# Three more transposes handed to the DMA rings, loads that queue behind them, and a new instruction order in a fused attention and channel-mix kernel

## The chip, the cores and the metric

The kernel runs on one core of a Trainium2 chip. The metric is device time in microseconds (us), the median of several executions. A profiled execution gives the trace that is read below.

## What is computed

Cut to what matters (B = 8 batches, H = 8 heads, S = 576 tokens, head width 64, so C = 512; F = 1024):

```python
kv  = einsum('bhsd,bhse->bhde', k, v)
u   = einsum('bhsd,bhde->bhse', q, kv)
x   = u / sqrt(mean(u * u, axis=-1) + 1e-6) * g_norm          # heads side by side: (B, S, C)
x_prev = x shifted by one token (zero in front)
xk  = mu_k * x + (1 - mu_k) * x_prev
xr  = mu_r * x + (1 - mu_r) * x_prev
km  = maximum(xk @ w_k, 0)                                     # (B, S, F)
out = 1 / (1 + exp(-(xr @ w_r))) * ((km * km) @ w_v)           # (B, S, C)
```

Inputs and output are float32 in memory; the matmuls work on bfloat16.

## The kernel before

**Stages of one batch.** The three inputs of a batch come by DMA from the queue of GpSimd (POOL), cast on the way (`load`, L189 to L194; word `ld.0`, `ld.1`, `ld.2` for k, v and q). TensorE (PE) makes `kv` (word `kv`, L278 to L288), which ScalarE (ACT) or VectorE (DVE) moves out of PSUM (`kvo`). q must be turned so that its channels lie on the partitions. Up to batch 3 that is 36 small PE transposes for each half of the heads (`qt`, L322 to L330), moved out by `qto`; from batch `QD = 4` on it is one transposing DMA on the queue of SyncE (SP) (`q_turn`, word `qd`, L299 to L302). Such a batch needs a swapped copy of `kv` as well (`kvs`, L295), and its `u` is made from 64x64 pieces (`u_turned`, L304, products on L316) in place of `u` (L342, products on L352).

Then come the squares of u (ACT, `sq`, L357), their sums (DVE, `red`, L361), a Newton iteration for the inverse root (DVE, `nw`, eight short steps) and the product (DVE, `mul`). The normalised rows must be turned back to have channels on the partitions: up to batch 4 by 36 PE transposes (`x` and `x0`, L435) moved out by `xo` and `x0o` with the factor g_norm; for batches in `YD = (5, 6, 7)` the product goes into the one tile `yd` (`mult_rows`, L399 and L403), a transposing DMA on SP's queue writes the tile `xT` (`y_turn`, word `yd`, L407 to L409), and `gx` (L411) multiplies by g_norm in place.

`xT` feeds `wrap` (L591), `dif` (L595), the scaled differences `sc` (L601 on ACT, L603 on DVE) and the sums `add` (L618) that give xk and xr. Then the channel mix: `K` (L631, four matmuls 128x288 and a relu for each of 8 blocks and 2 halves), `ks` (the squares, L639 or L637), `R` (L653, then a sigmoid, L656), `V` (L663, a group of four matmuls 128x512), `fin` (DVE product L676, then two stores on SP's queue, L684). The channel mix takes 128 tokens at a time, across the border of a pair of batches.

**The order.** A scheduler is switched off (`tc.manual_schedule()`). The string `ORDER` lists every step as a word; the loop on L791 to L796 issues them one by one, and each engine and each DMA queue works through its own instructions in that order, waiting by semaphores where data or a buffer is not ready. A quote mark after a word puts the step on DVE, else ACT, where there is a choice; the digits after `=` name the PSUM banks that the step takes. A bank is taken by the matmuls and given back by the step that reads it out last.

**Buffers.** k and q of even batches, and v, go into fixed tiles (`sq0`, `q0`, `qT0`), so the next even batch's load waits until the last reader is done; odd batches share one tile for each input (`in_k`, `in_v`, `in_q`). Working tiles come from a pool that hands out buffers of a tag in rotation: two for each tag of `mine` (L264), seven for `rt` (L645), six for `sig` (L655), seven for `out` (L675).

**The head and the tail.** Batch 0 and batch 1 have words of their own (`kvc`, `uc`, `Ka`, `Kz` for batch 0; `kvh`, `uh`, `xh` for the two halves of batch 1's heads). The last 128 tokens are made by `last_vv` (L666, words `L.0` and `L.1`), 256 columns at a time, with a product and two stores (one on SP's queue, one on ACT's) for each.

## Time and profile before

| | |
|---|---|
| Median of 3 runs | 199.24 us (198.97 to 199.28) |
| The profiled execution's own time | 198.45 us |
| Its span, first to last instruction | 196.7 us |
| PE busy | 185.8 us (94%) |
| DVE busy | 163.0 us (83%) |
| ACT busy | 134.1 us (68%) |
| POOL busy | 27.6 us (14%) |
| Bytes moved by DMA | 31.51 MB, mean 160 GB/s |

Times in views of the trace count from the first instruction. A line such as `L631` is a line of the kernel before; a busy PE is one with matmuls in flight, not one at its peak. A DMA's landing is when its completion semaphore reaches its full count; the instruction that issues it ends long before, save that a transposing DMA keeps its queue's engine for some us.

### The profile page before, as it was taken

How to read it: one execution, taken by the hardware profiler on the slowest of the kernel's cores; microseconds unless marked ns; L12 is line 12 of the kernel's file. 1: busy time of each engine (PE TensorE's matmuls, PEld its weight loads, DVE VectorE, ACT ScalarE, POOL GpSimd, SP SyncE). 2: the span in 40 equal slices, each digit the busy share in tenths (PEclk: the TensorE clock that was granted, in tenths of full speed). 3: DMA queues.
4: the chain of work that ended last, by engine and by line, in shares of the span. 5: the costliest groups of instructions: out<-in, count | busy, mean ns of one | idle time of the engine just before them, and what ended most of it. 6: DMA issues, size and time to landing. Idle time of an engine off the chain costs nothing.

```text
span 196.7 us, 5776 instructions
## 1 busy us (share of the span) xinstructions
PE 185.8 (94%) x2387; PEld 111.1 (56%) x2409; DVE 163.0 (83%) x356; ACT 134.1 (68%) x275; POOL 27.6 (14%) x44
## 2 busy tenths in 40 slices
PE   7788899999999999999999999999999999999991
PEld 2435565665564667567554775676445666764450
DVE  2488899996999999978999899899899997876241
ACT  2375898779969867969987658989855557532310
POOL 7953343004021004002100000000000000000000
PEclk9999999999999999999999999999999999999999
DMA  5999999999999998999999378335723842005654
GB/s 212 219 211 206 202 205 208 207 217 243 230 230 208 220 189 223 224 170 268 154 215 202 81 136 171 86 80 29 176 45 58 182 107 57 0 0 130 140 144 124
DMA packets 38030, 31.51 MB, mean 160 GB/s; under 512 B 18924, under 2 KB 32500, under 8 KB 38004
## 3 DMA queue, kind: packets, MB, share of 16 engines
q0 software_dynamic: 14400, 16.19, 49.3%
q1 hardware_dynamic: 23204, 14.43, 33.5%
q10 hardware_dynamic: 400, 0.52, 0.8%
q8 instruction: 19, 0.31, 0.6%
q14 instruction: 7, 0.06, 0.1%
HBM read 33.56 MB, written 9.44 MB: 219 GB/s over the span
## 4 chain that ended last, share of the span: by engine, by line
PE 80%; DVE 9%; DMA 4%; issue 2%; ACT 2%; SPq 0%; DVEq 0%; POOLq 0%
PE ps_v L663 28%; PE ps_km L631 28%; PE ps_r L653 15%; DMA q<-in_q_dram 3%; PE ps_kv L287 2%; PE ps_u L316 1%; DVE y L420 1%; PE ps_x L435 1%; DMA out_dram<-out_sb 1%; DVE xT L512 1%; DVE out_sb L676 1%; PE ps_u L352 1%; DVE ss L361 1%; DVE sqk L639 1%; PE ps_qt L330 1%
## 5 line engine op out<-in xcount | busy, mean ns | idle before, releaser
L663 PE MATMUL ps_v<-wv_sb,sqk 128*128 128x512 bf16 x266 | 64.8, 379 | 1.0 <-issue 0.3
L631 PE MATMUL ps_km<-xk,wk_sb 128*128 128x288 bf16 (+3 forms) x480 | 64.0, 285 | 0.0
L631 PEld LDWEIGHTS <-wk_sb 128*128 128x128 bf16 x480 | 45.7, 98 | 16.2
L663 PEld LDWEIGHTS <-sqk 128*128 128x128 bf16 x280 | 26.7, 98 | 29.5 <-issue 0.6
L623 ACT ACTIVATE rt<-ps_km 128x288 bf16<-128x288 f32 (+3 forms) x81 | 33.5, 427 | 12.6 <-PE ps_km L631 9.0
L653 PE MATMUL ps_r<-wr_sb,xr 128*128 128x512 bf16 x136 | 34.9, 379 | 0.5
L656 ACT ACTIVATE sig<-ps_r 128x512 bf16<-128x512 f32 x36 | 21.2, 596 | 18.9 <-PE ps_r L653 18.6
L676 DVE TENSOR_TENSOR out_sb<-ps_v,sig 128x512 f32<-128x512 f32 (+1 forms) x37 | 24.3, 670 | 9.3 <-PE ps_v L663 7.7
L637 ACT ACTIVATE sqk<-rt 128x576 bf16<-128x576 bf16 (+4 forms) x32 | 23.4, 746 | 4.4 <-DVE rt L625 4.2
L601 ACT ACTIVATE m<-dx,cols 128x576 bf16<-128x576 bf16 (+1 forms) x30 | 21.7, 756 | 4.2 <-DVE dx L595 4.0
L625 DVE TENSOR_SCALAR rt<-ps_km 128x288 bf16<-128x288 f32 (+3 forms) x39 | 17.8, 473 | 6.6 <-PE ps_km L631 5.0
L653 PEld LDWEIGHTS <-xr 128*128 128x128 bf16 x144 | 13.9, 98 | 14.2
L361 DVE TENSOR_REDUCE ss<-sq 128x16 f32<-128x1024 bf16 (+1 forms) x12 | 15.8, 1344 | 0.4 <-ACT sq L357 0.4
L357 ACT ACTIVATE sq<-ps_u 128x512 bf16<-128x512 f32 (+1 forms) x30 | 14.6, 556 | 0.0
L618 DVE TENSOR_TENSOR xr<-m,xT 128x1152 bf16<-128x1152 bf16 x16 | 11.9, 750 | 0.8 <-ACT m L601 0.8
L639 DVE TENSOR_TENSOR sqk<-rt 128x576 bf16<-128x576 bf16 (+3 forms) x25 | 11.7, 482 | 0.7 <-ACT rt L623 0.6
L595 DVE TENSOR_TENSOR dx<-xT 128x2304 bf16<-128x2304 bf16 (+5 forms) x13 | 11.4, 893 | 0.4
L603 DVE TENSOR_SCALAR m<-dx,cols 128x576 bf16<-128x576 bf16 (+3 forms) x36 | 11.4, 346 | 0.2
L618 DVE TENSOR_TENSOR xk<-m,xT 128x1152 bf16<-128x1152 bf16 (+2 forms) x16 | 10.9, 699 | 0.2
L420 DVE TENSOR_TENSOR y<-ps_u,rs 128x512 bf16<-128x512 f32 (+1 forms) x15 | 8.4, 628 | 0.1
L217 ACT CAST kv<-ps_kv 128x128 bf16<-128x128 f32 (+1 forms) x15 | 3.3, 244 | 6.9 <-PE ps_kv L472 5.7
L261 PE MATMUL ps_warm<-zeros 128*128 128x512 bf16 x18 | 6.9, 502 | 1.2 <-DVE eps L224 1.2
(91 smaller groups left out, 162.2 us busy)
## 6 DMA issues: line engine op xcount, KB each, us to landing
out_dram<-out_sb SPq DMA_DIRECT2D x67, 128.0 KB, 3.2
qT<-in_v_dram POOLq DMA_DIRECT2D x3, 576.0 KB, 14.4
sq<-in_k_dram POOLq DMA_DIRECT2D x3, 576.0 KB, 12.9
q<-in_q_dram POOLq DMA_DIRECT2D x3, 576.0 KB, 10.8
in_q<-in_q_dram POOLq DMA_DIRECT2D x3, 576.0 KB, 7.9
in_v<-in_v_dram POOLq DMA_DIRECT2D x3, 576.0 KB, 14.3
in_k<-in_k_dram POOLq DMA_DIRECT2D x3, 576.0 KB, 11.8
wk_sb<-in_moe_w_k_dram POOLq DMA_DIRECT2D x2, 512.0 KB, 9.1
```

The source lines that it names most:

```text
L357: ACT.activation(out=sq[:, rg(t0, n, i) if n else slice(0, 1)], in_=held["u", a, part, i][1], func=AF.Square)
L361: DVE.tensor_reduce(out=ss[:, g0:g1], in_=sq[:, g0:g1], op=ALU.add, axis=AX.X)
L601: eng.activation(out=out_, in_=in_, func=AF.Copy, scale=mu)
L618: DVE.tensor_add(out=dst, in0=m[:, hs, c0:c1], in1=x[:, hs, c0:c1])
L623: eng.activation(out=dst, in_=ps, func=AF.Relu)
L625: eng.tensor_scalar(out=dst, in0=ps, scalar1=0.0, scalar2=None, op0=ALU.max)
L631: nc.tensor.matmul(ps[:, n, :], wk_sb[:, cc, 128 * fc:128 * fc + 128], at[b]["xk"][:, cc, c0:c1], start=(cc == 0), stop=(cc == NHP - 1))
L637: eng.activation(out=sqk[:, fcs, o:o + n], in_=src, func=AF.Square)
L653: nc.tensor.matmul(ps, xr[:, cc, 128 * t:128 * t + 128], wr_sb[:, cc, :], start=(cc == 0), stop=(cc == NHP - 1))
L656: ACT.activation(out=sig[b, t], in_=give("r"), func=AF.Sigmoid)
L663: nc.tensor.matmul(ps, sqk[:, fc, 128 * t:128 * t + 128], wv_sb[:, fc, :], start=(fc == 0), stop=(fc == NFC - 1))
L676: DVE.tensor_mul(out=o, in0=give(key), in1=sig[b, t][:, c])
```

## The change

Five things change together.

1. `QD` goes from 4 to 3 and `YD` from (5, 6, 7) to (4, 5, 6, 7): batch 3's q and batch 4's y are turned by DMA and not by PE.
2. Each transposing DMA leaves a piece of its output in a list `turning`. The next `load` first copies two values from each such piece on GpSimd, so it waits for the landing of the transposing DMAs that stand ahead of it in the order, and so do all loads behind it on that queue. (A step `gate` that did such a copy for q alone, and that the order before did not use, is gone.)
3. Work tiles get names of their own: one buffer each for even and odd batches, and slots for `rt`, `sig` and `out` that are taken from a list of free ones and returned by the step that used them last. The counts stay 7, 6 and 7.
4. `last_vv` splits its columns 384 and 128 in place of 256 and 256, and the order does the 128 first.
5. The whole order is new, with the banks. It has 22 filler matmuls (`wm` and the 12 at the start) where there were 18.

The diff, the order cut to the places that are spoken of:

```diff
-    Kz.0.2 Kz.0.0 Kz.0.5' ... Ka.0.7=7 ... Kz.0.6 ... qt.1.0=50 Kz.0.3' ... Kz.0.7 ... kvh.0=41 kvho.0.0 Kp.0.1.1'=3
-    kvho.0.1 Kp.0.1.0'=2 uh.1.0=60 ...
+    fu.0.0.1.0.256 Kz.0.2' Ka.0.5=7 fu.0.0.3.0.256 sc.0.1.0' kvh.0=30 qto.1.0.1 kvho.0.1' qto.1.0.0 Kz.0.5'
+    kvho.0.0 uh.1.0=52 uh.0.0=14 ...
...
-    kv.2=26 ... ld.2.4 ... ld.0.4 ... kv.3=37 ... ld.1.4 qt.3.1=40 ... qt.3.0=21 ... ld.2.5 ... ld.0.5 ... ld.1.5 ... qd.4
+    kv.2=60 ... ld.0.4 ... ld.1.4 ... fin.0.3 fin.0.0 ... qt.2.0=47 qt.2.1=20 qd.3 ... fin.0.2 ... fin.0.1 ... kv.3=20
+    ... ld.2.4 ... ld.2.5 ... ld.0.5 ... ld.1.5 ... K.2.4.0=7 u.3.0=46 fin.1.4 qd.4 u.3.2=1 fin.1.7 u.3.1=23 ... kv.4=07
...
-    kv.4=02 ... ld.0.6 ... ld.1.6 ... u.4.0=41 u.4.1=35 ks.2.7 qd.5 ... ld.2.7 ... u.4.2=0 ... kv.5=67
+    fin.1.8 ... ld.2.6 ... qd.5 ... ld.1.6 ... V.2.1.0=6 kv.5=73 V.2.0.1 ... V.2.2.1 u.4.2=5 u.4.1=42 ... ld.0.6
...
-    x0.4=40 ... x0o.4.0 x.4.0.4=25 ... wrap.4 ... dif.4
+    mul.4.1.0 ... mul.4.1.1 ... mul.4.0.1 mul.4.0.0 ... u.5.1=21 u.5.0=67 u.5.2=0 K.3.3.0=4
+    mul.4.2.0 add.3.1.0 sq.5.0.1 ks.3.7' ... yd.4 ks.3.6' fin.2.3 R.3.6=3 red.5.5.9 ld.0.7
+    red.5.0.5 nw.5.0.1 ks.3.3 ld.1.7 R.3.4=5 R.3.5=4 nw.5.1.2 ... qd.6 ... ks.3.4' ... mul.5.0.1 ks.3.5 R.3.7=3
+    R.3.8=5 V.3.5.0=4 V.3.6.0=3 V.3.4.0=5 gx.4.0 mul.5.1.1
+    mul.5.0.0 mul.5.2.0 gx.4.1 mul.5.1.0 V.3.8.0=7 wrap.4 dif.4 sc.4.0.2 V.3.7.0=1 yd.5 sc.4.1.2' ... kv.6=60 ...
+    fin.3.4 ... add.4.0.0 add.4.0.1 ... K.4.1.1'=2 ld.2.7 ...
...
-    V.7.4.1 sta.7.5 V.7.7.0=4 fin.7.4 V.7.7.1 sta.7.6 fip.7.7 sta.7.7 L.0=2 L.1=6
+    V.7.6.1 fip.7.7 fin.7.4 R.7.8=0 fip.7.6 sta.7.6 sta.7.7 L.1=2 L.0=7
...
@@ load
             x_in[name, b] = {"k": sq0, "v": qT0, "q": q0}[name]
+        while turning:
+            nc.gpsimd.tensor_copy(out=passed, in_=turning.pop())
         nc.gpsimd.dma_start(out=x_in[name, b], in_=by_token(dram[name], b))
 
-    def gate(a):
-
-        nc.gpsimd.tensor_copy(out=passed, in_=at[a]["qT"][0:1, G - 1:G + 1, 0])
+    turning = []
...
@@ mine
-            at[a][key] = work.tile(shape, dtype, tag=tag or key, name=tag or key)
+            name = f"{tag or key}{key[1] if tag else a % 2}_"
+            at[a][key] = work.tile(shape, dtype, tag=name, name=name, bufs=1)
...
-    QD = 4
+    QD = 3
...
@@ q_turn
         nc.sync.dma_start_transpose(out=qT_, in_=x_in["q", a].rearrange("p m x -> p (m x)"))
+        turning.append(qT_[0:1, 0, 0:2])
...
-    YD = (5, 6, 7)
+    YD = (4, 5, 6, 7)
...
@@ y_turn
         nc.sync.dma_start_transpose(out=xT[a % 2].rearrange("p n (t x) -> p (n t) x", x=128), in_=yd.rearrange("p n t x -> p (n t x)"))
+        turning.append(xT[a % 2][0:1, 0:2, 0])
...
+    free = {"rt": list(range(7)), "sig": list(range(6)), "out": list(range(7))}
+    place = {}
+
+    def slot(kind, key, shape, dtype):
+
+        n = place[kind, key] = free[kind].pop(0)
+        return work.tile(shape, dtype, tag=f"{kind}{n}_", name=f"{kind}{n}_", bufs=1)
+
+    def leave(kind, key):
+        free[kind].append(place.pop((kind, key)))
...
-            rts[b, fc] = work.tile([128, S], BF16, tag="rt", name="rt", bufs=7)
+            rts[b, fc] = slot("rt", (b, fc), [128, S], BF16)
...
-        sig[b, t] = work.tile([128, C], BF16, tag="sig", name="sig", bufs=6)
+        sig[b, t] = slot("sig", (b, t), [128, C], BF16)
...
@@ last_vv
-        c = slice(C // 2 * part, C // 2 * part + C // 2)
+        c = (slice(0, 3 * C // 4), slice(3 * C // 4, C))[part]
...
@@ finish
-        o = outs[b, t] = work.tile([128, c.stop - c.start], FP32, tag="out", name="out_sb", bufs=7)
+        o = outs[b, t, c.start] = slot("out", (b, t, c.start), [128, c.stop - c.start], FP32)
...
@@ ops
-        "gate": lambda eng, a: gate(a),
...
-        "ks": lambda eng, b, fc: km_square(fc, S * (b % 2), rts[b, fc], eng),
+        "ks": lambda eng, b, fc: (km_square(fc, S * (b % 2), rts[b, fc], eng), leave("rt", (b, fc))),
```

## The prediction

> **What bounds the kernel now.** I read the page first: the busy rows and the slices.

> ```profile
> PE 185.8 (94%) x2387; PEld 111.1 (56%) x2409; DVE 163.0 (83%) x356; ACT 134.1 (68%) x275; POOL 27.6 (14%) x44
> ...
> DMA  5999999999999998999999378335723842005654
> ```

> PE is busy for 94% of the span; the DMA engines are full for its first half and half idle after. Then the windows, cut where PE stops waiting and where its last matmul ends (PE busy is the first number after the length):

> ```profile
> 0.00:21.90 21.90, 17.07 (x254) 8.67 (x254) 13.57 (x39) 11.92 (x25) 14.21 (x26) 1.00 1.05 211
> 21.90:192.40 170.50, 168.74 (x2134) 102.44 (x2156) 148.98 (x317) 122.19 (x251) 13.36 (x18) 1.00 0.83 155
> 192.40:196.70 4.30, 0.02 (x1) 0.00 (x0) 0.42 (x1) 0.00 (x0) 0.00 (x0) 0.92 0.45 124
> ```

> From 21.9 to 192.4 us PE idles for 170.50 - 168.74 = 1.8 us in all. In that stretch time can be won only by taking work off PE, and each wait that PE gets is paid in full. So the sum is: PE work removed, less the PE waits that the new order makes.

> What ends the head is a load. The timeline of POOL and PE, and the DMA view for that issue (last column: us to landing):

> ```profile
> 9.78 0.72 POOL L213 DMA_DIRECT2D in_v<-in_v_dram  x1
> ...
> in_v<-in_v_dram POOLq DMA_DIRECT2D x1, 288.0 KB, 12.0
> ...
> 21.90 0.48 PE L522 MATMUL ps_kv<-in_v,in_k 64*64 64x64 bf16 x36 [0.37 <-ACT qT L217]
> ```

> The first half of batch 1's v lands at 9.78 + 12.0 = 21.8 us, and `kvh.0`, which needs it, starts at 21.90. The loads of the head are issued in the same order in both kernels, so this time stays.

> **The change part by part.** The chain of waits gives the price of each PE step:

> ```profile
> 17.52 1.27 PE ps_km L708 x8
> ...
> 41.78 0.71 PE ps_kv L287 x72
> ...
> 56.71 0.65 PE ps_qt L330 x72
> ...
> 64.87 0.81 PE ps_u L352 x40
> ...
> 74.85 0.63 PE ps_x L435 x36
> ...
> 102.40 0.86 PE ps_r L653 x4
> 103.26 0.86 PE ps_v L663 x4
> ...
> 109.31 2.45 PE ps_km L631 x20
> ...
> 136.49 0.78 PE ps_u L316 x68
> ```

> *PE work removed.* Batch 3's q: 72 transposes, 0.65 us. Batch 4's y: 36 transposes, 0.63 us. Batch 3's `u` becomes the turned kind, 0.78 in place of 0.81. Together 1.3 us. With them go four `qto` and four `xo`/`x0o` on ACT and DVE, and two `kvs` and two `gx` come; both engines idle in part beside PE (windows: 149 and 122 of 170.5 us), so that is taken at nothing, unless one of them becomes the last to arrive (rivals).

> *The head.* Before, all `Kz` stand ahead of `kvh.0`; in the new order `Kz.0.5`, two of the L708 matmuls, comes behind it: 2 x 1.27 / 8 = 0.3 us later. Right behind that stands `uh.1.0`, which needs kv moved out of PSUM, where before 16 matmuls of L631 filled this time. Bounds for the wait: nothing, or the 0.37 us of the wait in the row of 21.90; I take 0.2. The four extra fillers lie in PE's idle 21.90 - 17.07 us: nothing, and if that cover were gone, under 1 us.

> *The tail.* The last product is 384 columns wide, not 256. Groups by shape:

> ```profile
> L676 DVE TENSOR_TENSOR out_sb<-ps_v,sig 128x512 f32<-128x512 f32 x35 | 23.5, 684 | 8.6 <-PE ps_v L663 7.7 <-issue 1.0
> ...
> L676 DVE TENSOR_TENSOR out_sb<-ps_v,sig 128x256 f32<-128x256 f32 x2 | 0.8, 424 | 0.6 <-DMA out_dram<-out_sb 0.5 <-PE ps_v L671 0.2
> ```

> Halfway between 424 and 684 ns: +0.13 us. The matmuls have the same columns in all.

> *Named tiles.* Batches alternate as in the rotation, and the slots stay 7, 6 and 7: nothing; it removes no wait, since PE has next to none on them.

> *The waits of the loads.* POOL waits, and what queues behind is only loads. SP is not made to wait, but each transposing DMA holds it, and behind stand stores. What counts is whether kv and u find their data. The rows (timelines of SP, POOL and PE, one line of the chain, DMA landings):

> ```profile
> 28.63 0.74 POOL L194 DMA_DIRECT2D in_q<-in_q_dram  x1 [1.56 <-PE ps_x L435]
> ...
> in_q<-in_q_dram POOLq DMA_DIRECT2D x1, 576.0 KB, 17.4
> ...
> 59.15 0.77 POOL L194 DMA_DIRECT2D in_v<-in_v_dram  x1
> ...
> in_v<-in_v_dram POOLq DMA_DIRECT2D x1, 576.0 KB, 14.3
> ...
> 63.01 7.81 SPq L302 DMA_TRANSPOSE qT<-q  x1
> ...
> 75.39 0.74 POOL L194 DMA_DIRECT2D q<-in_q_dram  x1 [15.48 <-DMA qT<-q]
> ...
> 77.10 9.88 SPq L302 DMA_TRANSPOSE qT<-in_q  x1
> ...
> 92.04 0.74 POOL L194 DMA_DIRECT2D in_q<-in_q_dram  x1 [14.41 <-DMA qT<-in_q]
> ...
> in_q<-in_q_dram POOLq DMA_DIRECT2D x1, 576.0 KB, 6.6
> ...
> 90.20 0.77 PE L287 MATMUL ps_kv<-in_v,in_k 64*64 64x64 bf16 x68
> ...
> 99.27 0.44 PE ps_u L316 x30
> ...
> 111.87 3.00 SPq L409 DMA_TRANSPOSE xT<-yd  x1
> ...
> xT<-yd SPq DMA_TRANSPOSE x1, 6.6
> ...
> 149.83 3.00 SPq L409 DMA_TRANSPOSE xT<-yd  x1
> ...
> xT<-yd SPq DMA_TRANSPOSE x1, 4.9
> ```

> Beside loads a transposing DMA takes 75.4 - 63.0 = 12.4 and 92.0 - 77.1 = 14.9 us to land (a load waited for it each time); with no load in flight 6.6 and 4.9 us. [...]

> *Will v of batch 5 be there?* `qd.3` goes out when q of batch 3 lands, 28.63 + 17.4 = 46.0. Four loads are then in flight, where the row of 14.9 us had three, so I bound it by 12.4 and 18: landed at 58.4 to 64.0. Then `ld.2.4` goes out, and v of batch 5 three issues of some 0.75 later, 60.6 to 66.2; it lands 14.3 us on, 75 to 80.5. `kv.5` in the new order: before, 48.4 us lie between `kv.2` (41.8) and `kv.5` (at 90.2). The new order has between them two `R`, three `V`, nine `K` (0.49 each), one pair of `qt` and one batch's plain `u` less, and two `Kp` of about 0.65 more: 48.4 - 1.7 - 2.6 - 4.4 - 0.65 - 0.8 + 1.3 = 39.5. With the head's 0.5 that is 41.8 + 0.5 + 39.5 = 81.8, 1 to 7 us after the data. I take no wait.

> *And the turned y of batch 4?* Here everything is closer. `u.4` ends at about 81.8 + 0.7 + 1.7 (two `V`) + 0.8 = 85. From the end of u to the issue of `yd` the kernel before took 111.87 - 99.7 = 12.2 us in batch 5 and 149.83 - 137.3 = 12.6 in batch 7. In the new order DVE has little foreign work between, so I take 11: `yd.4` goes out at 96 (95 to 97.5) and lands 4.9 to 6.6 later, at 101 to 103. DVE then works through this, the groups by shape giving ns:

> ```profile
> L618 DVE TENSOR_TENSOR xk<-m,xT 128x1152 bf16<-128x1152 bf16 x12 | 8.7, 751 | 0.0
> L595 DVE TENSOR_TENSOR dx<-xT 128x2304 bf16<-128x2304 bf16 x6 | 8.1, 1357 | 0.3
> L399 DVE TENSOR_TENSOR yd<-ps_u,rs 128x512 bf16<-128x512 f32 x12 | 7.7, 684 | 0.1
> ...
> L403 DVE TENSOR_TENSOR yd<-ps_u,rs 64x256 bf16<-64x256 f32 x6 | 2.5, 422 | 0.1
> ...
> L603 DVE TENSOR_SCALAR m<-dx,cols 128x576 bf16<-128x576 bf16 x27 | 9.1, 363 | 0.1
> ...
> L591 DVE COPY xT<-xT 128x252 bf16<-128x252 bf16 x8 | 2.0, 250 | 0.2
> ```

> The products of batch 5 first, since they write the one `yd` tile that the DMA reads (4 x 0.68 + 2 x 0.42 = 3.6), then `wrap` 0.25, `dif` 1.36, four `sc` 1.45, one `fin` 0.68, two `add` 1.5: 8.8 us from the landing to the first `K` of batch 4. PE reaches that `K` at about 111.4: before, `K.4.1.1` is the second group after 109.31, so 109.8; between `kv.2` and it the new order has a `kv`, two `Kp` and two `V` more (3.7), and a `qt` pair, an `R`, a `K` and the `x` steps less (2.6); the head adds 0.5. So the turned y must land by 102.6, against 101 to 103: less than 1 us to spare at the middle. I take no wait, but this is the thinnest place. [...]

> **Sum.** -1.3 + 0.3 + 0.2 + 0.1 = -0.7 us. The profiled execution takes 198.45 (span 196.7 and 1.75 around it), so 197.75 for one like it. The median of the runs is 0.8 above the profiled one; the same -0.7 gives 198.5.

> **The rivals.**

> *A, the turned y comes late (slower).* DVE stands at batch 5's first product until `yd.4` has landed, then `K.4` waits for xk. It decides when that landing is later than 102.6. For it: loads of batch 6 go out when `qd.5` lands, and if any is still in flight, the rows say 12.4 to 14.9 us in place of 4.9 to 6.6. Against it: `qd.5` has one load beside it, not three. Priced between 6.6 and 12.4: 9.5 us, landing at 105.5, 2.9 late; -0.7 + 2.9 = +2.2, 201.4 us. At the far bound, 12.4, it is 5.8 late and 204.3.

> *B, the waiting loads themselves cost (slower).* While loads wait, the rings run empty: the first load after such a wait took 6.6 us to land. If four loads and `qd.4` stretch v's 14.3 by one more load of about 3 us, v lands at up to 83.5, `kv.5` waits 1.7, and `u.4` shares that wait: -0.7 + 1.7 = +1.0, 200.2 us. [...] No run so far shows the waits.

> *C, the gain is used up (same).* Waits of 0.3 to 1.1 us spread over the new order, by the rows' 0.2 to 0.4 each: 198.9 to 199.6.

> *D, more than the sum.* The new order also removes part of the 1.8 us that PE idles now: -1.3 - 0.5, 197.4 us.

> **How the numbers follow.** A difference of about 0.2% (0.4 us) is what a measurement of this kernel can tell. Forecast, all data in time: 0.38 (198.1 to 198.8). D 0.07. C 0.13. A 0.27. B 0.15. Faster 0.45, same 0.13, slower 0.42. Low end 197.4 (D); high end A's 201.4, with a quarter of A's chance beyond it. The forecast's own range is 198.1 to 198.8.

> **What would show it.** Right: no PE wait over 0.5 us after 22 us, the PE sum smaller by about 1.3 us, PE's last matmul near 191.6. `in_v` of batch 5 landing before `kv.5` and `yd.4` landing within 6.6 us would confirm the two margins. A: a PE wait on `ps_km` L631's successor near 111, ended by DVE xk, with DVE waiting on the transposing DMA. B: a PE wait on `ps_kv` or `ps_u` near 82 to 85 that ends at a DMA. Wrong altogether: a wait in the head between 22 and 42 us, or ACT as the last to arrive there.

## The result: 0.8% slower, and the profile after

| | before | after |
|---|---|---|
| Median of 17 runs of each on the same chip | 198.94 us (197.86 to 199.35) | 200.28 us (199.34 to 205.35) |
| Ratio | | 1.0077, 95% interval 1.0054 to 1.0101 |
| Profiled execution, its own time | 198.45 us | 199.34 us |
| Span | 196.7 us | 197.5 us |

A run over 1.5% above the fastest of its kernel, here the one of 205.35, is left out of every ratio, here and below, while the medians are of all runs.

The forecast was 198.5 (0.7 under the 199.24 of the first three runs of the old kernel). Measured: 1.3 us slower by the medians of 17, 0.9 by the profiled executions. Line numbers move in the new kernel: K is L633, V L675, R L665, the turned `u` L317, `kv` L287, the products into `yd` L400 and L404, `add` L620; in the experiments they move by a line or two more.

From the page of the new kernel: the busy row, the slices of the DMA engines, and the queue that carries instructions (packets, MB, share).

```profile
PE 185.3 (94%) x2314; PEld 110.0 (56%) x2337; DVE 160.5 (81%) x351; ACT 131.5 (67%) x277; POOL 28.9 (15%) x50
...
DMA  6999999999999999999999998884916422022865
...
q8 instruction: 18, 0.29, 0.6%
```

The busy rows look alike, and the DMA engines are now busy at 80% or more from slice 2 up to slice 27 of 40, before up to slice 22. The difference is in the stretches, cut as in the prediction with one more stretch around PE's longest wait:

```profile
0.00:21.68 21.68, 17.48 (x254) 9.00 (x256) 12.81 (x39) 12.31 (x25) 13.65 (x26) 1.00 1.05 211
21.68:65.88 44.20, 43.61 (x724) 25.60 (x734) 40.54 (x89) 33.66 (x73) 9.12 (x13) 1.00 1.18 207
65.88:72.11 6.23, 4.99 (x149) 3.84 (x140) 5.92 (x11) 5.15 (x15) 0.00 (x0) 1.00 1.14 215
72.11:193.16 121.05, 119.23 (x1207) 71.52 (x1223) 100.63 (x214) 80.38 (x167) 6.15 (x11) 1.00 0.79 142
193.16:197.50 4.34, 0.00 (x1) 0.00 (x0) 0.56 (x1) 0.00 (x0) 0.00 (x0) 0.75 0.48 121
```

Between head and tail PE is busy for 43.61 + 4.99 + 119.23 = 167.83 us in place of 168.74, and that part is 171.48 long in place of 170.50. So 0.9 us of PE work is gone and 1.9 us of PE idleness has come (some 22 matmul records are missing from each of the two traces, which makes a few tenths of either uncertain). The head is 0.2 shorter, the tail 0.04 longer. PE's waits from 22 to 193 us:

```profile
PE ps_km L633 <- issue: 1.2, 1, 1.2
PE ps_v L675 <- issue: 0.9, 6, 0.2
PE ps_r L665 <- ACT sq__3051 L358: 0.3, 1, 0.3
```

The row of V is mostly short holes where records are missing. The first row is one wait of 1.24 us, and nothing released it: `issue` means that no semaphore event explains it. PE's timeline there:

```profile
65.49 0.83 PE L317 MATMUL ps_u<-kv__1292,qT__1115 64*64 64x64 bf16 x72
66.28 0.84 PE L287 MATMUL ps_kv<-qT,sq 64*64 64x64 bf16 x72
67.06 3.81 PE L633 MATMUL ps_km<-xk__1455,wk_sb 128*128 128x288 bf16 x29
72.11 1.03 PE L633 MATMUL ps_km<-xk__1455,wk_sb 128*128 128x288 bf16 x7 [1.24 <-issue]
```

It falls inside a group of four `K` matmuls, after the first, where it has nothing left to wait for: `K` groups ahead of it had used the same tokens, and its bank was taken by its first matmul. Just before it stand the turned `u` of batch 3 and the `kv` of batch 4, 72 small matmuls and 72 weight loads each: 288 instructions in 1.6 us.

Last, the chain of waits where the prediction had its thinnest margin:

```profile
95.19 8.40 DMA xT<-yd
...
103.68 1.89 DVE yd L400 x3
...
110.46 1.43 DVE xk__2503 L620 x2
...
111.93 1.14 PE ps_km L633 x8
```

The turned y of batch 4 landed at 103.6, one us after the 102.6 of the prediction, and DVE then ran with hardly a pause into the first `K` of batch 4. PE, itself 1.2 us late, waited 0.13 us for it.

### The profile page after: what moved, and what is told of

Its sections match the earlier page's. It is cut to its first block, busy times and chain, and to the rows that moved or that the text cites. A ratio compares the mean times of both kernels' runs of the same rounds, so it can differ in the third digit from the quotient of the medians.

```text
span 197.5 us, 5653 instructions
## 1 busy us (share of the span) xinstructions
PE 185.3 (94%) x2314; PEld 110.0 (56%) x2337; DVE 160.5 (81%) x351; ACT 131.5 (67%) x277; POOL 28.9 (15%) x50
## 4 chain that ended last, share of the span: by engine, by line
PE 76%; DMA 14%; DVE 4%; issue 2%; ACT 1%; POOL 1%; DVEq 0%; POOLq 0%
PE ps_km L633 30%; PE ps_v L675 25%; PE ps_r L665 14%; DMA in_v<-in_v_dram 6%; DMA xT<-yd 4%; DMA q<-in_q_dram 3%; PE ps_u L317 2%; PE ps_kv L287 2%; DVE yd L400 1%; PE ps_x L437 1%; PE ps_v L683 1%; ACT sq__3051 L358 1%; DVE xk__2503 L620 1%; DVE dx__2403 L597 1%; PE ps_qt L331 1%
## 5 line engine op out<-in xcount | busy, mean ns | idle before, releaser
L675 PE MATMUL ps_v<-wv_sb,sqk 128*128 128x512 bf16 x263 | 63.3, 379 | 1.4 <-issue 0.9
L633 PEld LDWEIGHTS <-wk_sb 128*128 128x128 bf16 x480 | 45.7, 98 | 18.3 <-issue 2.0
L675 PEld LDWEIGHTS <-sqk 128*128 128x128 bf16 x280 | 26.5, 98 | 28.6 <-ACT sqk L639 0.2
L665 PE MATMUL ps_r<-wr_sb,xr 128*128 128x512 bf16 x139 | 34.6, 379 | 0.6 <-ACT sq__3051 L358 0.3
L665 PEld LDWEIGHTS <-xr 128*128 128x128 bf16 x144 | 13.9, 98 | 15.3 <-DVE xr L620 0.8
L625 ACT ACTIVATE rt<-ps_km 128x384 bf16<-128x384 f32 (+2 forms) x19 | 9.0, 492 | 3.0 <-PE ps_km L633 1.6
L633 PE MATMUL ps_km<-xk__1455,wk_sb 128*128 128x288 bf16 x64 | 8.8, 286 | 1.2 <-issue 1.2
L633 PE MATMUL ps_km<-xk__2841,wk_sb 128*128 128x288 bf16 x64 | 9.0, 286 | 0.1
L633 PE MATMUL ps_km<-xk__869,wk_sb 128*128 128x192 bf16 (+1 forms) x64 | 8.9, 287 | 0.0
L633 PE MATMUL ps_km<-xk__3378,wk_sb 128*128 128x288 bf16 x64 | 8.8, 286 | 0.0
L633 PE MATMUL ps_km<-xk__2503,wk_sb 128*128 128x288 bf16 x64 | 8.5, 286 | 0.1
L633 PE MATMUL ps_km<-xk__1965,wk_sb 128*128 128x288 bf16 x64 | 8.4, 286 | 0.0
L633 PE MATMUL ps_km<-xk__3218,wk_sb 128*128 128x288 bf16 x64 | 8.3, 286 | 0.0
L427 ACT ACTIVATE xT<-xT,cols 128x1152 bf16<-128x1152 bf16 x5 | 6.0, 1245 | 0.5 <-DMA xT<-yd 0.5
L724 PE MATMUL ps_km<-xk__373,wk_sb 128*128 128x320 bf16 x32 | 5.5, 299 | 0.5 <-ACT rs L510 0.4
L427 ACT ACTIVATE xT<-ps_x,cols 128x256 bf16<-128x256 bf16 (+3 forms) x12 | 5.0, 469 | 0.6 <-PE ps_x L437 0.5
L429 DVE TENSOR_SCALAR xT<-ps_x,cols 128x1024 bf16<-128x1024 bf16 (+3 forms) x8 | 3.6, 466 | 1.6 <-PE ps_x L437 1.6
L260 PEld LDWEIGHTS <-zeros 128*128 128x128 bf16 x22 | 2.3, 114 | 4.5 <-issue 2.2
L641 DVE TENSOR_TENSOR sqk<-rt 128x1280 bf16<-128x1280 bf16 (+3 forms) x6 | 4.4, 727 | 0.1
L194 POOL COPY passed<-xT 1x2 bf16<-1x2 bf16 x2 | 0.6, 319 | 26.1 <-DMA xT<-yd 26.1
L724 PEld LDWEIGHTS <-wk_sb 128*128 128x128 bf16 x32 | 2.9, 97 | 2.4 <-issue 1.2
## 6 DMA issues: line engine op xcount, KB each, us to landing
qT<-in_v_dram POOLq DMA_DIRECT2D x3, 576.0 KB, 14.9
sq<-in_k_dram POOLq DMA_DIRECT2D x3, 576.0 KB, 14.7
q<-in_q_dram POOLq DMA_DIRECT2D x3, 576.0 KB, 8.4
in_q<-in_q_dram POOLq DMA_DIRECT2D x3, 576.0 KB, 10.9
in_k<-in_k_dram POOLq DMA_DIRECT2D x3, 576.0 KB, 14.3
in_v<-in_v_dram POOLq DMA_DIRECT2D x3, 576.0 KB, 17.1
sqk<-in_k_dram SPq DMA_DIRECT2D x1, 576.0 KB
```

The costliest lines, as they stand in the source:

```text
L260: nc.tensor.matmul(ps, zeros[:, :128], zeros, start=True, stop=True)
L427: eng.activation(out=dst, in_=src, func=AF.Copy, scale=g_sb)
L429: eng.tensor_scalar(out=dst, in0=src, scalar1=g_sb, scalar2=None, op0=ALU.mult)
L625: eng.activation(out=dst, in_=ps, func=AF.Relu)
L633: nc.tensor.matmul(ps[:, n, :], wk_sb[:, cc, 128 * fc:128 * fc + 128], at[b]["xk"][:, cc, c0:c1], start=(cc == 0), stop=(cc == NHP - 1))
L641: eng.tensor_mul(out=sqk[:, fcs, o:o + n], in0=src, in1=src)
```

## The experiments

The theory they test, I (instruction supply): PE's instructions come by DMA in pieces. The page shows 18 packets of 0.29 / 18 MB = 16 KB for 2 x 2337 = 4674 records of PE, about 260 each; the waits below fix it at 256. The theory's own assumption is that a piece is asked for when PE enters the one before it (what the traces show is the packet, which moved 2.1 to 4.6 us after that point in the table below), so that PE runs dry if it uses 256 instructions faster than the next piece arrives. K, R and V groups use 8 in 0.5 to 0.86 us; `u` and `kv` use 288 in 1.6 us. Its rivals: A (turned y late) and B (waits of the loads) of the prediction, L (v of batch 5 late), and that the wait belongs to its place. All ratios are to the old kernel, with 95% intervals.

### The parts of the change, one at a time

**kv of batch 4 a little later**

```diff
-    u.3.1=23 sq.3.0.0 kv.4=07 ... kvo.4.1 kvo.4.0 ... K.2.0.1=7
+    u.3.1=23 sq.3.0.0 ... K.2.0.1=7 kv.4=07 kvo.4.1 kvo.4.0
```

> The changed kernel with kv.4 and its two kvo moved five K groups later, so that the 72 small matmuls of u.3 and the 72 of kv.4 no longer stand side by side. Theory I (PE ran out of instructions: its idle 1.24 us at 70.9 lies inside one group of four K matmuls and ends at nothing that the trace shows): that idle time vanishes and, if it was on the path, the run is 1.2 us shorter than the changed kernel. Theory D (the chain of loads and transposing DMAs sets the pace: v of batch 5 landed at 81.98 and kv.5 began at 82.02): the idle time vanishes, but kv.5 waits about 1 us for v instead, and the run is within 0.3 us of the changed kernel.

Measured: 200.51, 1.0104 [1.0058, 1.0151]. The wait of 1.24 was not there. But the edit made waits of its own, for PSUM banks that `fin`, `K` and `kvo` had not yet given back (0.4 us at 67, 0.4 at 70, 0.6 at 71), so PE came there later. The first row below is a wait that ends at 128.1, not one of these.

```profile
PE ps_km L632 <- ACT rt__2882 L624: 0.7, 1, 0.7
PE ps_km L632 <- issue: 0.6, 1, 0.6
PE ps_km L632 <- ACT kv__1621 L215: 0.6, 1, 0.6
PE ps_km L632 <- DVE out__1574 L687: 0.4, 1, 0.4
```

The `issue` row is a new wait at 87.8, after `kv.5` and `u.4`, which stand 2 us apart: a place that theory I would name. The vanished wait itself proves nothing here, and the time is inconclusive.

**A second `yd` tile**, so that DVE's products of batch 5 need not wait for the DMA that reads batch 4's.

```diff
-    yd = const.tile(...)
+    yds = [const.tile(...) for n in range(2)]      # batch a uses yds[a % 2]
```

> The changed kernel with a yd tile each for even and odd batches, so batch 5's products need not wait until batch 4's transposing DMA has read the one tile. Theory Y (DVE stood from about 101 to 103.7 at that product and the first K of batch 4 waits for what DVE does after it): DVE does the products 2 to 3 us earlier, xk of batch 4 is ready up to 3 us earlier, K.4 does not wait; in the changed kernel's profile K.4 waited only 0.13 us, so the profile gains 0.1 to 0.3 us and the median, whose runs are up to 1 us longer than the profiled one, up to 1 us. Theory D alone: no change, the landing of yd.4 itself is what counts.

Measured: 199.91, 1.0079 [1.0039, 1.0118]: no gain that can be told. K of batch 4 no longer waited, but `issue` took 2.2 us (1.5 at 71.3 and 0.65 at 88.2). So the product chain behind the turned y is not, by itself, what cost 1.3 us.

**No waits of the loads**

```diff
-        while turning:
-            nc.gpsimd.tensor_copy(out=passed, in_=turning.pop())
```

> The changed kernel without the copies that make loads wait for the transposing DMAs ahead of them; loads then wait for their buffers alone. If the waits of the loads cost time by themselves: q of batch 4 goes out at about 46 instead of 62.7, v of batch 5 lands about 3 us earlier (79), and the run is 0.5 to 1.5 us shorter. If the waits help (a transposing DMA beside loads takes 12 to 15 us instead of 5 to 8): qd.5 and yd.4 land 3 us or more later, u.5 or K.4 wait, and the run is 1 to 4 us longer.

Measured: 210.91, 1.0595 [1.0546, 1.0644], far more than the 1 to 4 us expected. The chain and PE's waits say why: with five loads in flight beside it the turned y took 16.5 us, and a PSUM bank that DVE's next product would have read out held PE for 7.8. The last row is from POOL's timeline.

```profile
95.69 16.51 DMA xT<-yd
...
PE ps_v L673 <- DVE yd L398: 7.8, 1, 7.8
...
67.10 0.74 POOL L193 DMA_DIRECT2D in_q<-in_q_dram  x1 [19.85 <-DMA qT__1115<-in_q]
```

Rival B, that the waiting loads themselves cost, is refuted: in this order their waits are worth over 10 us (210.91 against the new kernel's 200.28). Nor did they hold up v of batch 5: without them its q still waited until `qd.3` had read the tile `in_q`, and v went out at 68.6 in place of 64.9.

**Loads of batch 5 as k, v, q**

```diff
-    ld.2.5 ... ld.0.5 ... ld.1.5          (q, k, v)
+    ld.0.5 ... ld.1.5 ld.2.5              (k, v, q)
```

> The changed kernel with the loads of batch 5 in the order k, v, q in place of q, k, v. Theory D: v of batch 5 lands one load (3 to 4 us) before 81.98, q as much later, and kv.5 never waits; with the idle 1.24 us at 70.9 still there the profiled run stays within 0.3 us, the median gains up to 0.7 us if slower runs are slow because v is late. Theory I: no change at all.

Measured: 201.72, 1.0173 [1.0127, 1.0218]. v of batch 5 came 4.3 us earlier (77.7), but q, needed by `qd.5`, came last; everything in the chain of loads behind it slipped, k of batch 6 landed at 103.1, and the turned y beside it at 105.8. Rival A shows itself, 1.4 us at a V whose bank DVE should have read out:

```profile
PE ps_km L632 <- issue: 1.8, 1, 1.8
PE ps_v L674 <- DVE yd L399: 1.4, 1, 1.4
```

**y of batch 4 by PE again** (`YD = (5, 6, 7)`, 36 transposes and their moves put back):

```diff
-    YD = (4, 5, 6, 7)    ... yd.4 ... gx.4.0 ... gx.4.1
+    YD = (5, 6, 7)       ... x.4.0.4=35 ... xo.4.0.4.1' xo.4.0.4.0 ... x0.4=34 x0o.4.0 x0o.4.1'
```

> The changed kernel with batch 4's y turned on PE again (36 transposes, moved out by DVE and ACT), the rest of its order kept. Theory D (yd.4 landed at 103.6 and held up batch 5's products and the first K of batch 4): those waits go, at the price of 0.63 us of PE work; 0 to 0.5 us longer in a run like the changed kernel's profiled one, up to 1 us shorter in its median. Theory I: the idle time at 71 us stays, the run is 0.6 us longer.

Measured: 202.51, 1.0183 [1.0150, 1.0215]. The `issue` waits stayed (1.8 at 70.9, 0.5 at 88.0), and the transposes put in by hand made two waits of 0.8 near 102. So the fourth y by DMA is not what makes the `issue` waits, and this order has no room for its PE form; what the fourth y costs or gains cannot be told from this run.

**q of batch 3 by PE again** (`QD = 4`):

```diff
-    QD = 3    qd.3 ... kvs.3.0 ... kvs.3.1
+    QD = 4    ... qt.3.0=57 ... qto.3.0.0 qto.3.0.1 qt.3.1=46 ... qto.3.1.0 qto.3.1.1'
```

> The changed kernel with batch 3's q turned on PE again (72 transposes, four moves out of PSUM) and u.3 made in 40 products in place of 72. Theory I (PE's instructions come over the DMA engines in pieces of 256; u.3 turned and kv.4 side by side are 288 instructions in 1.6 us, and PE used them up before the next piece was there): with 224 in their place the idle 1.24 us near 71 shrinks by half or vanishes. Theory D: with qd.3 gone the loads of batch 5 no longer wait for it, v of batch 5 lands 3 us or more before 82, and kv.5 and what follows never wait. Both: 0.65 us of PE work more, up to 1.5 us of waits less; -1 to +0.5 us against the changed kernel. If neither cause holds: +0.7 us.

Measured: 203.66, 1.0224 [1.0170, 1.0279]. `u` of batch 3 is plain again (40 matmuls, not 72), and the wait near 71 is gone. But `kv.3`, `x` of batch 2 and `qt` of batch 3 now stand close together at 58 to 61 us, and there a wait without a releaser came, 2.2 us long. The next fences give windows up to the end of the wait, of the new kernel and of this one, then this one's around the wait (the third number from the end is the granted clock). The wait ended after 987 weight loads, that of the new kernel after 1114: 127 apart, or one piece of 256 to within a pair (each weight load has a matmul).

```profile
0.00:72.10 72.10, 66.08 (x1107) 38.44 (x1114) 59.26 (x137) 51.12 (x110) 22.77 (x39) 1.00 1.14 209
```

```profile
0.00:63.70 63.70, 57.47 (x979) 32.51 (x987) 51.17 (x124) 44.80 (x95) 22.57 (x38) 1.00 1.13 210
```

```profile
61.50:63.70 2.20, 0.04 (x1) 0.00 (x0) 2.10 (x5) 2.20 (x5) 2.08 (x3) 1.00 0.62 99
63.70:68.20 4.50, 4.49 (x14) 1.67 (x15) 1.07 (x2) 2.04 (x4) 0.00 (x0) 0.63 1.12 190
```

After the wait the granted clock was down to 0.63 for 4.5 us, which cost an estimated 1.5 us more (14 matmuls of V where 21 of 0.216 us, a quarter of a V group of 0.86, would fit). So the 203.66 is not the price of q by PE, but of the place where it was put.

**The two parts of q, put into the old kernel**: `QD = 3` alone, then also `kv.4` right behind the turned `u` of batch 3.

```diff
-    QD = 4    ... qt.3.1=40 ... qt.3.0=21 qto...
+    QD = 3    ... qt.2.0=72 qd.3 ... kvs.3.0 kvs.3.1'
```

> The kernel before with one part of the change alone: QD = 3, so batch 3's q is turned by DMA, its qd right after qt.2, the rest of the old order kept; kv.4 stands some 7 us behind u.3 as before. Theory I: no idle time over 0.3 us near u.3, so the 0.65 us of PE work shows as gain: 0.4 to 0.7 us shorter than before, unless u.3 waits for the transposing DMA. If the moved transposes do not pay at all: same as before.

> The same kernel as the one with QD = 3 alone, but with kv.4 moved up to stand right behind u.3, as in the changed kernel; the loads come as they did. Theory I: an idle stretch of PE of 0.5 to 2 us that nothing in the trace ends, within 5 us behind kv.4, inside a group of matmuls, and the run 0.5 to 2 us longer than with QD = 3 alone. If the idle time in the changed kernel came from its loads or buffers: no such stretch; at most kv.4 waits for its v, which the trace would name.

Measured: 199.72, 1.0034 [1.0010, 1.0057] and 199.98, 1.0053 [1.0033, 1.0073]. A third q by DMA, without anything else, costs the old kernel 0.3%, where a gain of 0.4 to 0.7 us was expected: `u` of batch 3 waited 0.8 us for it.

```profile
PE ps_u L315 <- DMA qT<-in_q: 0.8, 1, 0.8
```

The second is no test of I: its one profiled execution took 204.50, far over the median, and `u` waited for its q there too, which by theory I gives the next piece time to arrive before `u` starts. Inconclusive.

### Instruction supply, tested

**When the pieces came.** The traces keep the start and the length of each packet of the instruction queue q8. In the new kernel none starts from 65.8 to 69.4 us and one in the tenth of a us after that (first row: DMA view, 69.4 to 69.5); with the loads held back, an edit that follows below, one starts at 68.7 (second row: 68.6 to 68.7).

```profile
q8 instruction: 1, 0.02, 65.0%
...
q8 instruction: 1, 0.02, 54.9%
```

The same times for the boundary at 1114 weight loads, and, for the old kernel and the one with q of batch 3 by PE, at about 987 (us; the mark is one piece, 128 weight loads, ahead of the boundary):

| kernel | PE passes the mark | the packet moves | PE goes on | wait |
|---|---|---|---|---|
| new kernel | 65.9 | 69.5 to 70.5 | 72.1 | 1.24 |
| new kernel once more | 66.1 | 70.4 to 71.4 | 72.8 | 1.80 |
| q of batch 3 by PE | 58.1 | 61.4 to 62.3 | 63.7 | 2.18 |
| old kernel | 56.4 | 59.9 to 60.8 | 62.3 | 0.12 |
| kv of batch 4 some 7 us behind u | 65.9 | 70.5 to 71.6 | 74.5 | none |
| loads of batch 5 later | 66.5 | 68.7 to 69.5 | 71.3 | none |
| twelve warm-up matmuls less | 66.7 | 70.8 to 71.7 | 73.1 | none |

In all the kept traces, the 15 waits of 0.2 us or more after 22 us that are put down to `issue` ended 1.3 to 1.6 us after the end of such a packet. That is what PE waited for. With loads in flight the packet started 3.3 to 4.6 us after the mark, with the loads of batch 5 held back 2.1 us after it.

**The new kernel once more**, for a second profiled execution.

> The new kernel unchanged, a second profiled execution. Theory I: the waits without a releaser lie again exactly 256 PE records behind a mark (near 71, and perhaps near 88 or 128, where other executions showed them), with lengths that differ by some 0.5 us since they depend on how the pieces fall among the loads' packets. That would also explain why the runs lie 0.9 us above the first profiled execution. If instead the wait near 71 were the only one of its kind, the second profile repeats the first within 0.2 us.

Measured: 201.18, 1.0124 [1.0091, 1.0157]; profiled 200.07. PE waited 1.8 us at 71.05 and 0.2 at 88.12, both without a releaser. All its records are there, and between the ends of the two waits lie exactly 256 matmuls and 256 weight loads, two pieces. The kernel is the same as in the result, and its ratio was 1.0077 there: ratios of different sessions that lie half a per cent apart are not to be told from each other.

```profile
PE ps_km L633 <- issue: 2.0, 2, 1.8
...
72.83:88.32 15.49, 15.28 (x256) 9.05 (x256) 12.78 (x27) 13.09 (x30) 0.92 (x2) 1.00 1.24 200
```

**kv of batch 4 some 7 us behind u**

```diff
-    u.3.1=23 ... kv.4=07 ... K.2.6.0=5
+    u.3.1=23 ... K.2.6.0=5 kv.4=04 ... K.2.3.0=5 kvo.4.1 kvo.4.0
```

> The new kernel with kv of batch 4 (and its moves out of PSUM) nine K, two R and two more K behind the turned u of batch 3, some 7 us, in place of directly behind it (2.45 us in the earlier spread). Theory I (PE's instructions come in pieces of 256, a piece is asked for when PE enters the one before, and takes 5.4 to 7 us to arrive beside loads): the piece that begins in the middle of u then lasts over 6.5 us, so the wait of 1.24 us near 71 is gone (under 0.3 in all between 65 and 78). PE is then 1.2 us earlier and kv of batch 5 wants its v at 80.8, which lands at 82.0: a wait of some 1.2 us ended by the load comes in its place (theory L, loads late), so the time stays within 0.5 of 200.3, unless v lands earlier too. Rival (the wait near 71 belongs to those K groups themselves, or to a record that the profile does not show): it stays, at K.2.1.0 or near 71, about 1.2 us.

Measured: 200.86, 1.0094 [1.0062, 1.0125]; profiled 199.47. As I and L had it: the packet was no earlier, PE needed it later, no `issue` wait is left, and PE, earlier, waits for v of batch 5, which landed at 82.25. Beside the new kernel of the same session (1.0124) no gain can be told.

```profile
PE ps_kv L286 <- DMA in_v<-in_v_dram: 0.9, 1, 0.9
PE ps_km L632 <- DVE out__1574 L687: 0.4, 1, 0.4
```

**u and kv side by side, but the loads of batch 5 later**

```diff
-    ld.2.5 ... ld.0.5 ... ld.1.5 ... kvo.4.1 kvo.4.0
+    kvo.4.1 kvo.4.0 ld.2.5 ld.0.5 ld.1.5
...
+        if b == 5 and name == "q":      # wait for kvo of batch 4
+            for e in range(2):
+                nc.gpsimd.tensor_copy(out=passed, in_=at[4]["kv"][0:1, 0, e, 0:2])
-        while turning:
+        while turning and b != 5:
```

(`b != 5` keeps these loads from waiting for `qd.4`, which they now follow in the order.)

> The new kernel with the three loads of batch 5 held back until kv of batch 4 is out of PSUM (POOL copies two of its values first), so that from 63 to 68 only the load of q of batch 4 is in flight beside u and kv. Theory I with the part that the pieces share the DMA engines with the loads: the piece for PE arrives within some 4 us in place of 6.2, and the wait near 71 falls from 1.24 to under 0.3 us with u and kv still next to each other. If the pieces take 6 us whatever else is in flight, the wait stays at 1.0 to 1.3. In both cases v of batch 5 is then issued at about 69 and lands 10 to 14 us later, 79 to 83: kv of batch 5 waits 0 to 2.5 us, so the time itself is 199.5 to 202 and tells little.

Measured: 201.31, 1.0121 [1.0071, 1.0171]; profiled 200.39. PE's timeline has no hole behind the 288 instructions:

```profile
66.17 0.83 PE L319 MATMUL ps_u<-kv__1292,qT__1115 64*64 64x64 bf16 x72
66.90 1.03 PE L289 MATMUL ps_kv<-qT,sq 64*64 64x64 bf16 x72
67.86 4.58 PE L635 MATMUL ps_km<-xk__1451,wk_sb 128*128 128x288 bf16 x36
72.28 1.89 PE L667 MATMUL ps_r<-wr_sb,xr 128*128 128x512 bf16 x8
```

With one load in flight in place of four the packet started 2.1 us after the mark, in place of 3.6 and 4.4, and the piece came in time. So the loads in flight are what made the piece late here. The price moved to where L had it: v of batch 5 landed at 83.2 and PE waited 1.6 us for it.

**The order untouched, twelve warm-up matmuls less**: 24 records fewer, 50 us earlier.

```diff
-    warm(12)      ... wm.2.4=4 ... wm.4.5=5
+    warm(4)       ... wm.1.4=4 ... wm.1.5=5
```

> The new kernel, order of the work untouched, with twelve warm-up matmuls less in the head (12 at the start become 4, four of the ten fillers go): 24 PE records fewer 50 us before the wait near 71. Theory I: the piece that was entered 52 records ahead of the end of u is now entered 28 records ahead of it, so 84 in place of 60 of its 256 records are K and R groups, 1.5 us more; the wait near 71 shrinks from 1.2 to 1.8 us to 0.4 or less and moves three groups on, to the first R of batch 2; the time falls by 0.8 to 1.3 us to about 199.2, if the head does not grow. Rival, that the wait belongs to the place (that K group, its bank, its data): it stays at the same group with 1.2 us or more.

Measured: 200.36, 1.0096 [1.0062, 1.0129]; profiled 199.04. No wait near 71; the same steps at the same place run through, and v of batch 5 (0.4 us) and the head (0.6 us at `uh`, a new wait) take part of the gain back. The packet was no faster, 4.1 us after the mark, but PE got to the boundary only 6.4 us after the mark, not 5.0. What moved the wait is a count, not a place: this is the clearest of the tests. The median stayed at 200.4 us, where about 199.2 was expected.

```profile
66.20 0.83 PE L316 MATMUL ps_u<-kv__1280,qT__1103 64*64 64x64 bf16 x72
67.04 0.79 PE L286 MATMUL ps_kv<-qT,sq 64*64 64x64 bf16 x72
67.76 4.61 PE L632 MATMUL ps_km<-xk__1443,wk_sb 128*128 128x288 bf16 x36
72.21 1.89 PE L664 MATMUL ps_r<-wr_sb,xr 128*128 128x512 bf16 x8
```

### Does a mended order beat the old kernel?

**kv of batch 4 apart, kv of batch 5 one V later, two `yd` tiles**

```diff
+    (kv.4 apart and two yd tiles as above)
-    V.2.1.0=6 kv.5=73 V.2.0.1
+    V.2.1.0=6 V.2.0.1 kv.5=73
```

> As the kernel with kv of batch 4 apart, with kv of batch 5 one V later and a second yd tile, so that the products of batch 5 do not wait for the turned y of batch 4. If the wait near 71 and the one at K of batch 4 are what keeps the new kernel above the old one, it gains 0.5 to 1.3 us on the new one: 199.0 to 199.8, near the old kernel's 198.9. If other waits take their place (v of batch 5 landing at 82, a piece running out near 88 where kv and u of the next batches stand 2 us apart), it stays at 200.0 to 200.8.

Measured: 199.78, 1.0036 [1.0014, 1.0057]; profiled 198.43 with a span of 196.7, the old kernel's to 0.02 us. The best of the new orders, and clear of the new kernel's 1.0124 [1.0091, 1.0157] of the same session, but not below the old one.

**Other banks and a K ahead of an R; then ten warm-up matmuls less; then a V ahead of kv of batch 5**

```diff
-    K.2.7.0=5 K.2.4.1=7 K.2.2.0=0 ...    R.5.5=3 K.5.0.0=7
+    K.2.7.0=7 K.2.4.1=0 K.2.2.0=5 ...    K.5.0.0=7 R.5.5=3
-    warm(12)  wm.2.4=4  wm.4.5=5                (second and third)
+    warm(6)   wm.1.4=4  wm.1.5=5
-    V.2.0.1 kv.5=73 ... V.2.1.1                 (third)
+    V.2.0.1 V.2.1.1 kv.5=73
```

> As the kernel with kv of batch 4 apart and two yd tiles, with other PSUM banks for the K groups behind u of batch 3 (the first of them waited 0.4 us for the bank that DVE's finish had held) and with one K of batch 5 ahead of its first R (which waited 0.3 us and 0.8 us at its weight load for xr from DVE). If both waits are gone and nothing replaces them, its profiled execution is 0.6 to 0.8 us under the 198.43 of the kernel without them, and the median some 0.6 under 199.78, 199.2. If v of batch 5 (landed at 81.5, 0.2 before its use) is then what PE waits for, only 0.3 us of it are left.

> As the kernel with other banks, with ten warm-up matmuls less in the head (12 at the start become 6, four of the ten fillers go), which moves every 256-instruction piece of PE by 20 records against the stages. Theory I: of the piece that now runs out near 85 to 87 (0.8 us in all, slow K groups behind u of batch 4), 57 records instead of 37 are then K groups, so it lasts 1.2 us longer and the wait there is gone: 0.5 to 0.8 us less than the kernel it is made from. Rival: the head needs the warm-ups (clock), and it grows by over 0.5 us; or the slow K groups are not from instruction supply and stay.

> As the kernel with ten warm-up matmuls less, with one more V of batch 2 ahead of kv of batch 5 (0.86 us), so that v of batch 5, landing at 81.5 to 82, is there when kv comes. If the late v is what most executions wait for beyond the profiled one, the median falls by 0.3 to 0.8 us against the kernel it is made from; if u of batch 4, 0.86 us later, makes its turned y late, K of batch 4 waits and it is no faster.

Measured: 200.71, 200.44 and 201.14 (ratios 1.0077 [1.0050, 1.0104], 1.0078 [1.0054, 1.0102], 1.0112 [1.0082, 1.0141]): all miss what was hoped. The new banks made a wait of their own (0.6 us at an R). With ten warm-up matmuls less the `issue` wait of the first one was gone, as theory I had it, but a wait of 0.7 us at `uh` in the head came. The first one's profiled execution, 201.19, is worth reading, since it caught rival A at work. Its chain and PE's waits:

```profile
95.69 11.39 DMA xT<-yd
107.08 0.02 issue
107.10 2.41 ACT xT L427 x2
...
112.92 1.43 DVE xk__2505 L620 x2
...
PE ps_km L633 <- DVE xk__2505 L620: 1.1, 2, 0.8
PE ps_r L665 <- DVE rt__1632 L627: 0.6, 1, 0.6
PE ps_km L633 <- issue: 0.6, 1, 0.6
```

Issued at 95.7, half a us later than in the new kernel, `yd.4` took 11.4 us here, against 8.4 there: the loads of v and k of batch 6 went out at 92.1 and 92.8, 2.3 us later than in the new kernel, and k landed at 104.5 in place of 101.2.

**The loads of k and v of batch 6 left out; and all loads kept, with two `yd` tiles** (both on the kernel with twelve warm-up matmuls less).

```diff
+        if b == 6 and name in "kv":                  (first)
+            return
         nc.gpsimd.dma_start(out=x_in[name, b], in_=by_token(dram[name], b))
```

> As the new kernel with twelve warm-up matmuls less, and the loads of k and v of batch 6 left out (its kv is built from what batch 4 left in those buffers, so batch 6 of the output is not the reference's): the turned y of batch 4 then has no load beside it. Rival A of the prediction, in the executions that were not profiled: the 199.0 to 200.9 of the kernel it is made from come from how late that y lands (it took 7 to 11 us beside those two loads). Then yd of batch 4 lands within 6.6 us of its issue, K of batch 4 does not wait, the runs lie within 0.8 us of each other, and the median falls from 200.4 to 199.2 or less. If the runs still spread over 1.5 us and the median stays above 199.8, the spread has another cause.

> As the new kernel with twelve warm-up matmuls less, with a second yd tile, all loads there: the products of batch 5 do not wait for the turned y of batch 4, so DVE is nearly 4 us ahead when it lands, and a landing up to 106 instead of 103 costs K of batch 4 nothing. If the late y sets the spread and DVE's products are half of the damage, the median falls by 0.3 to 0.7 us against 200.4; it is still above the old kernel's 198.9, since v of batch 5 and the head cost 1 us. If nothing changes, the y is not what PE waits for in most executions.

Measured: 199.53, 1.0031 [1.0011, 1.0050], and 199.94, 1.0069 [1.0040, 1.0097], against 1.0096 [1.0062, 1.0129] of the kernel that both are made from. Without the two loads y of batch 4 landed 5.7 us after its issue, and the ratio fell by 0.65%; its interval does not touch that of the kernel it is made from, which was measured in another session, but overlaps that of the second, measured beside it. But the runs still lay 1.6 us apart (198.4 to 200.0, leaving out one of 203.07). So late y is probably part of the spread, and not all of it. Two `yd` tiles alone cannot be told from none. In the first one's profile a wait of 0.4 us without a releaser came back, at the second R of batch 2, three groups on (the expectation for the kernel with twelve warm-up matmuls less had named the first R). It ended after 1114 weight loads, the very count of the new kernel's wait at a K:

```profile
0.00:74.61 74.61, 66.24 (x1107) 39.11 (x1114) 60.30 (x142) 52.53 (x114) 22.74 (x39) 1.00 1.13 207
...
PE ps_r L666 <- issue: 0.4, 1, 0.4
```

## Why the prediction was wrong

**PE work removed: the size held.** -1.3 and +0.3 for `Kz` were forecast between head and tail, 0.9 less was measured.

**Head: a little better.** +0.5 was forecast (0.3 inside the PE sum), but PE's first long stretch starts 0.2 earlier and nothing from 22 to 42 us waits over 0.2; why is open. **Tail: right in its product.** The last product took 0.56 in place of 0.42, +0.14 against +0.13; the tail as a whole grew by 0.04 only.

**The step that failed: "less the PE waits that the new order makes".** Between head and tail the prediction put this term at nothing, and PE's idleness there grew by 1.9 us: 1.24 is the one wait at 71, 0.13 the wait at `K` of batch 4, the rest in pieces of 0.3 us and less. The prediction looked for such waits at semaphores only: does the data land in time, does an engine come last. It placed the turned `u` of batch 3 and the `kv` of batch 4 side by side without pricing that, because each step alone was priced (0.78 and 0.71 us). Together they use up a piece of instructions in 1.6 us while four loads are in flight (DMA share 1.14 from 65.88 to 72.11), and PE waited 1.2 and 1.8 us in the two profiled executions. The old kernel knew this wait too, but with 0.1 us, ended at 62.25 us after 988 weight loads, within one of the 987 of the wait with q by PE (window of the old kernel up to there):

```profile
0.00:62.25 62.25, 56.85 (x981) 32.66 (x988) 50.74 (x123) 45.39 (x96) 23.11 (x38) 1.00 1.15 215
```

Its `u` of batch 3 was plain, and `kv.4` stood 9 us behind it. That it is supply is shown by the packets, which end 1.3 to 1.6 us ahead of the end of each such wait, and by four edits: the wait goes when the cluster is spread by 7 us, when the loads are held back, or when 24 records are taken out 50 us earlier, and it comes one piece earlier with the cluster of q by PE. That a piece is 256 instructions is borne out by the 18 packets for 4674 records, by the 127 weight loads between the waits of two kernels, and by the 256 matmuls and 256 weight loads between two waits of one. Most boundaries cost PE nothing that its waits show: from 22 to 193 us the new kernel's first profile has one `issue` wait over 0.2 us, the 1.24; the longest of any kernel, with q of batch 3 by PE, is 2.2.

**v of batch 5: forecast 75 to 80.5, needed 81.8; landed 82.0.** The load took 17.1 us and not the 14.3 of the row used, as the last of four loads issued one behind the other. That is the stretch that rival B priced, by one more load, but not B's cause: without the waits of the loads v went out later still. In the profile it cost nothing, only because PE had lost 1.2 us at 71; in four kernels where the wait at 71 was mended, it took 0.2 to 0.9 us. So the two are not a sum: mending either alone gives little, which fits that the kernel with kv of batch 4 apart stayed where it was. PE reached `kv.5` at 82.0 and the first `K` of batch 4 at 111.4, close to the 81.8 and 111.4 of the prediction, but with that unforeseen wait inside: by subtraction it would have come some 1.2 us earlier, and both margins were that much smaller than they looked. That B's 200.2 lies next to the measured 200.28 is luck too: its sign, a wait at `ps_kv` or `ps_u` near 82 to 85, is in neither profile of the new kernel.

**Turned y of batch 4: forecast 101 to 103, needed by 102.6; landed 103.6.** It took 8.4 us where the prediction took 4.9 to 6.6, while k of batch 6 was still in flight until 101.2; the rows of 4.9 and 6.6 had no load beside them. Rival A was named rightly as the thinnest place and priced at 2.9 us. It cost 0.13 in the profile of the new kernel, 1.4 and 1.1 in those of two variants, and taking its neighbours away took 0.65% off the ratio, with the reserve said there.

**Loads' waits.** In this order they are worth 10 us. That they also lengthen the chain of load, turn, load is seen in the order k, v, q: `qd.5` is issued 0.6 us later and y lands 2.2 later.

**What stays open.** The median of the new order lies 0.9 us above its first profiled execution, the old kernel's 0.5. Late y may account for some of that; to know, one would need traces of those runs. Whether some order with these transposes beats the old one is also open: the best tried came to 1.0036.

## What to carry to other kernels

Count instructions as well as microseconds: where two stages of small matmuls stand next to each other, ask how long PE takes for 256 instructions there, and what loads are in flight just then (here, where PE waited, it went on 5.6 to 6.7 us after passing the mark). A wait put down to `issue` inside one group of matmuls is the sign, and a test is cheap: take some instructions away far ahead and see whether it moves. Work removed from the bounding engine is worth its price only if every chain that feeds it has that much slack; here three chains, the pieces of instructions, v of batch 5 and the turned y of batch 4, had less than 1 us or none.
